# Spreading attention denominators over partitions: a DMA broadcast through DRAM in place of a TensorE matmul

## The chip, the cores and the metric

One NeuronCore of one Trainium2 chip runs the whole program. The metric is the device time of one execution in microseconds (us). "Faster" and "slower" mean by more than 2%. The kernel before takes 255.7 us.

A program on one core shows no second die to compare with, so the state of a run ("fast" or "slow") is told by its distance from the fastest run of the same kernel. A ratio is the mean time of one kernel's fast runs over that of the other's fast runs of the same rounds on the same chip, so it is not quite the ratio of the medians that are quoted.

## The reference, cut to what matters

```python
B, S, D, H = 1, 2048, 448, 16          # Dh = 28; N = 4 segments of L = 512
xn = layernorm(x)
for s in range(4):                      # attention with a memory carried from segment to segment
    p     = softmax(qs @ ks.T * scale + causal_mask)
    a_dot = p @ vs                                    # the kernel divides after the product
    num, den = phi(qs) @ M, phi(qs) @ z + 1e-6        # memory read
    o = g * num / den + (1 - g) * a_dot               # g = sigmoid(beta), per head
    M, z = M + phi(ks).T @ vs, z + sum(phi(ks))
out = x + (o @ wo) * silu((gelu(xn @ w_gate) * (xn @ w_up)) @ w_down)
```

Two divisions matter here: the softmax's, and `num / den`. The kernel does both late, as multiplications by inverses. Its products have 128 partitions = 4 heads x 32 rows (28 values, a denominator, padding) and 512 columns (tokens). The inverse of a head's 512 denominators is needed on all 32 partitions of that head.

## The kernel before: the parts that matter

```python
def evac(s, g, side, ps, copy=None):        # PSUM product to SBUF; its denominator rows by DMA to dc
    ...
    nc.sync.dma_start(out=dc[s, side][g * HG * RC:(g + 1) * HG * RC, :],
                      in_=t[Dh:P:HP, :].rearrange("i (c f) -> i c f", f=64))

def invert(s, side, g0=0, g1=G, to=None, eng=None, queues=None):
    ...                                     # VectorE: d = 1 / ((d + eps) * gate), 128 x 64, f32
    t = work.tile([P, 3, 64], BF16, name="terms")
    for i in range(3):                      # f32 as a sum of three bf16 terms
        eng.tensor_copy(out=t[p, i, :], in_=d)
        if i < 2:
            eng.tensor_tensor(out=d, in0=d, in1=t[p, i, :], op=ALU.subtract)
        queues[i].dma_start(out=rows[...][32 * i + g0 * HG:32 * i + g1 * HG, :]
                            .rearrange("h (c f) -> h c f", f=64), in_=t[p, i, :])

def inverses(s, side, g, at):               # TensorE spreads 4 heads' rows over 4 x 32 partitions
    r = ps_m.tile([P, L], F32, name="m")
    nc.tensor.matmul(out=r[:], lhsT=spread[:, g, :], rhs=rows[at][:], start=True, stop=True)
    return r[:]

# used by VectorE, 27 times:
nc.vector.tensor_tensor(out=dst, in0=o_n, in1=inverses(s, 1, g, 1), op=ALU.mult)   # scale_memory ("scl")
nc.vector.tensor_tensor(out=o_a, in0=o_a, in1=r, op=ALU.mult)                      # combine ("cmb")
# normalised x, one buffer per block of 128 tokens, transposed by DMA:
xn[b] = xns[b]                              # 4 buffers
nc.sync.dma_start_transpose(out=xnT[s][:, :, b * P:(b + 1) * P], in_=xn[b][:])
# the plan: in which slot of the program each small step is issued, found by search for this kernel
PLAN = {..., "inv3": 138, "cmb30": 144, "cmb31": 147, "cmb32": 149, ...}
```

The program goes: gate phase 0, attention 0, gate 1, attention 1, gates 2 and 3, attention 2, attention 3, the rest of the down projections and the output. A "gate phase" is the gate and up projections of one segment.

## Time and profile before

| | |
|---|---|
| time | 255.7 us (255.2 to 255.8) |
| TensorE, VectorE, ScalarE, GpSimd busy | 93%, 71%, 66%, 36% of a span of 253.9 us |
| chain that ended last | TensorE 75% |
| DMA | 15.07 MB, 27509 packets |

Read the chain first: it follows the work back from the last instruction, and its shares tell which engine's work made the time. Busy shares only tell which engines could not have been the limit. The lines themselves stand in the prediction.

### The profile page before, as it was taken

Reading aid. Unit: us, or ns where it says so; the run is one execution under the profiler, and the core shown is the slowest. Engines: PE = TensorE matmul, PEld = TensorE weight load, DVE = VectorE, ACT = ScalarE, POOL = GpSimd, SP = SyncE. Lnnn points to the kernel's source line nnn. Section 1 sums busy time; section 2 is a strip of 40 time slices with the busy share of each in tenths; the row PEclk is TensorE's granted clock in tenths of the full one; section 3 lists DMA queues with packets and bytes.
Section 4 is the critical chain, followed back from the end, with each engine's and each line's share of the span. In section 5 each row is a group of like instructions: output and inputs, shape, how many; then the busy total and the mean of one; then the engine's idle time right before and its main releaser. Section 6 shows DMA issues by size and latency. Waiting matters only on the chain.

```text
span 253.9 us, 4494 instructions
## 1 busy us (share of the span) xinstructions
PE 237.1 (93%) x1589; PEld 103.6 (41%) x1609; DVE 180.7 (71%) x362; ACT 167.5 (66%) x248; POOL 90.6 (36%) x195
## 2 busy tenths in 40 slices
PE   7899999999999999999999999999998999989970
PEld 7443333444344435444434334434433333334630
DVE  5877554827986857976698557536799866796990
ACT  5755878679995657679883575333897888884100
POOL 2500653443631322444532107040174545482030
PEclk9999999999999999999999999999999999999995
DMA  7999413200220135020120220000200010001111
GB/s 213 329 313 261 82 23 65 91 25 4 43 45 6 37 63 148 1 59 5 40 61 1 49 41 4 4 8 3 76 16 23 26 27 6 6 1 28 54 38 48
DMA packets 27509, 15.07 MB, mean 59 GB/s; under 512 B 17880, under 2 KB 26584, under 8 KB 27480
## 3 DMA queue, kind: packets, MB, share of 16 engines
q1 hardware_dynamic: 25276, 12.93, 20.6%
q10 hardware_dynamic: 2204, 1.79, 2.4%
q8 instruction: 14, 0.23, 0.4%
q14 instruction: 15, 0.12, 0.2%
HBM read 9.18 MB, written 1.84 MB: 43 GB/s over the span
## 4 chain that ended last, share of the span: by engine, by line
PE 75%; DVE 9%; ACT 7%; issue 4%; DMA 1%; POOL 1%; ACTq 0%
PE s L648 19%; PE m L689 15%; PE m L402 9%; PE s L496 5%; ACT pt L502 4%; PE pv L648 4%; PE m L648 4%; PE pv L515 4%; PE s L655 3%; PE m L441 3%; PE m L724 3%; PE m L573 2%; PE m L655 2%; DMA x_sb<-in_A_x_dram 1%; DVE hT L662 1%
## 5 line engine op out<-in xcount | busy, mean ns | idle before, releaser
L502 ACT ACTIVATE pt<-s 128x1024 bf16<-128x1024 f32 x80 | 77.5, 1024 | 16.1 <-PE s L496 12.6
L506 POOL TENSOR_SCALAR_AFFINE_SELECT pt<-pt 128x256 bf16<-128x256 bf16 x128 | 55.3, 452 | 63.4 <-ACT pt L502 60.4
L689 PE MATMUL m<-wd_sb,hT 128*128 128x448 bf16 x224 | 50.5, 353 | 0.2 <-DVE wu_sb L613 0.2
L662 DVE TENSOR_TENSOR hT<-gl,s 128x512 bf16<-128x512 bf16 x40 | 27.0, 680 | 9.0 <-ACT gl L661 8.6
L648 PE MATMUL s<-xnT,wg_sb 128*128 128x512 bf16 x118 | 32.3, 380 | 0.9 <-DVE hT L662 0.4
L648 PE MATMUL s<-xnT,wu_sb 128*128 128x512 bf16 x118 | 32.0, 379 | 0.1
L661 ACT ACTIVATE gl<-s 128x512 bf16<-128x512 f32 x40 | 23.7, 593 | 10.2 <-PE s L648 8.5
L689 PEld LDWEIGHTS <-hT 128*128 128x128 bf16 x224 | 20.4, 98 | 22.0 <-issue 4.0
L662 DVE TENSOR_TENSOR hT<-gl,pv 128x512 bf16<-128x512 bf16 x16 | 11.0, 688 | 24.9 <-ACT gl L661 24.9
L648 PEld LDWEIGHTS <-wu_sb 128*128 128x128 bf16 x168 | 16.4, 98 | 19.9 <-issue 0.2
L648 PEld LDWEIGHTS <-wg_sb 128*128 128x128 bf16 x168 | 15.2, 98 | 21.5 <-issue 6.0
L661 ACT ACTIVATE gl<-m 128x512 bf16<-128x512 f32 x16 | 9.4, 589 | 19.1 <-PE pv L655 19.1
L496 PE MATMUL s<-qT,kT 32*128 32x512 bf16 (+3 forms) x256 | 19.4, 300 | 1.9 <-ACT pt L502 1.9
L295 POOL TENSOR_TENSOR rstd<-rstd,nhalf 128x2 f32<-128x2 f32 (+1 forms) x8 | 5.4, 677 | 40.0 <-DVE rstd L293 40.0
L315 ACT ACTIVATE xn<-x_sb,shift,rstd 128x448 bf16<-128x448 bf16 (+1 forms) x24 | 12.7, 590 | 7.7 <-DVE shift L312 7.7
L402 PE MATMUL m<-xnT,wk_pad 128*128 128x512 bf16 x58 | 16.3, 379 | 1.1 <-DVE sg L727 0.5
L402 PE MATMUL m<-xnT,wq_pad 128*128 128x512 bf16 x60 | 16.6, 380 | 0.2
L441 PE MATMUL m<-wv_sb,xnT 128*128 128x448 bf16 x64 | 14.4, 353 | 1.3 <-DVE vaug L443 1.2
L695 ACT ACTIVATE th<-m 128x448 f32<-128x448 f32 x16 | 8.8, 550 | 8.6 <-PE m L689 8.6
L406 DVE CAST kT<-m 128x512 bf16<-128x512 f32 x16 | 10.9, 683 | 4.9 <-PE m L402 4.7
L496 PEld LDWEIGHTS <-kT 32*128 32x128 bf16 x256 | 5.6, 91 | 19.7 <-issue 19.3
L515 PE MATMUL pv<-pt,vaug 128*32 128x128 bf16 (+3 forms) x256 | 13.5, 303 | 0.0
(138 smaller groups left out, 360.6 us busy)
## 6 DMA issues: line engine op xcount, KB each, us to landing
x_sb<-in_A_x_dram SPq DMA_DIRECT2D x7, 224.0 KB
wd_sb<-in_B_w_down_dram SPq DMA_DIRECT2D x1, 1568.0 KB
wg_sb<-in_B_w_gate_dram SPq DMA_DIRECT2D x1, 1344.0 KB
wu_sb<-in_B_w_up_dram SPq DMA_DIRECT2D x1, 1344.0 KB
xr<-in_A_x_dram ACTq DMA_DIRECT2D x2, 448.0 KB
out_dram<-o_out SPq DMA_DIRECT2D x8, 112.0 KB
out_dram<-wq_pad SPq DMA_DIRECT2D x4, 112.0 KB
wo_sb<-in_A_wo_dram SPq DMA_DIRECT2D x4, 98.0 KB
```

Of the source, the lines that this page charges most:

```text
L315: nc.scalar.activation(out=xn[b][:, o], in_=xs[:, b, c], func=ACT.Identity, scale=rstd[:, b:b + 1], bias=shift[:])
L402: nc.tensor.matmul(out=pr[:], lhsT=wpad[nm][:, c, g * HG:(g + 1) * HG, :].rearrange("p h d -> p (h d)"), rhs=xnT[s][:, c, :], start=(c == ...
L441: nc.tensor.matmul(out=vp[:, 0:D], lhsT=xnT[s][:, c, b * P:(b + 1) * P], rhs=wv_sb[:, c, :], start=(c == 0), stop=(c == NDC - 1))
L496: nc.tensor.matmul(out=sp[i // 2][:, i % 2, c0:c0 + n], lhsT=kT[s][r, g, kb * P:(kb + 1) * P], rhs=qT[s][r, g, kb * P:L], start=True, stop ...
L502: nc.scalar.activation(out=pt[:, :, 0:w], in_=sp[pr][:, :, 0:w], func=ACT.Exp, scale=scale)
L506: nc.gpsimd.affine_select(out=v, in_=v, pattern=[[0, 2], [1, P]], compare_op=ALU.is_ge, fill=0.0, base=0, channel_multiplier=-1)
L515: nc.tensor.matmul(out=acc[i * HP:(i + 1) * HP, kb * P:L], lhsT=vaug[s % 2][:, kb, g * HG + i, :], rhs=pts[i // 2][:, i % 2, c0:c0 + n], s ...
L648: nc.tensor.matmul(out=gu[fc][i], lhsT=w_sb[:, c, fc * P:(fc + 1) * P], rhs=xnT[s][:, c, :], start=start and c == 0, stop=not start and c ...
L655: nc.tensor.matmul(out=gu[fc][i], lhsT=wg_sb[rs, NDC - 1, fc * P:(fc + 1) * P], rhs=xnT[s][rs, NDC - 1, :], start=start, stop=not start)
L661: nc.scalar.activation(out=gl[:], in_=g, func=ACT.Gelu_apprx_tanh)
L662: nc.vector.tensor_tensor(out=hT[s][:, fc, :], in0=gl[:], in1=u, op=ALU.mult)
L689: nc.tensor.matmul(out=d_ps[:, 0:D], lhsT=hT[s][:, fc, b * P:(b + 1) * P], rhs=wd_sb[:, fc, :], start=(fc == 0), stop=(fc == NFC - 1))
```

## The change

Intent: take 27 matmuls off the busiest engine. The f32 inverses go to a DRAM tile in one DMA, and each group's four rows are fetched into a 128 x 512 f32 tile in SBUF, every row read 32 times, up to three tiles ahead. To make room: three xn buffers in place of four, two output buffers in place of three, a late `unit` matrix. The closing multiplies and adds are reordered, and the plan is a new one. Cut to its core:

```diff
-    rows = [const.tile([P, L], BF16, name=f"rows{i}") for i in range(2)]
-    spread = const.tile([P, G, P], BF16, name="spread")
+    SPREAD = 3
+    sprp = pool("sprp", SPREAD)
+    drp = pool("drp", 3, space=DRAM)
@@ invert
-    (three bf16 terms, three DMAs to rows)
+    nc.sync.dma_start(out=t[g0 * HG:g1 * HG, :].rearrange("h (c f) -> (h c) f", f=64), in_=d)
+    for g in range(g0, g1):
+        wanted.append((plan[f"{'scl' if side else 'cmb'}{s}{g}"], len(wanted), s, side, g, t))
+    fetch()
+def fetch():
+    while wanted and len(spread) < SPREAD:
+        w = min(wanted)
+        wanted.remove(w)
+        s, side, g, t = w[2:]
+        b = spread[s, side, g] = sprp.tile([P, L], F32, name="spread")
+        nc.sync.dma_start(
+            out=b[:],
+            in_=t[g * HG:(g + 1) * HG, :].unsqueeze(1).to_broadcast([HG, HP, L]))
@@ inverses
-    nc.tensor.matmul(out=r[:], lhsT=spread[:, g, :], rhs=rows[at][:], start=True, stop=True)
+    return spread[s, side, g][:]        # after its use: spread.pop(...), fetch()
@@ normalised x
-    for i in range(NB):                 # xn buffers
+    for i in range(NB - 1):
-    xn[b] = xns[b]
+    xn[b] = xns[b % len(xns)]
@@ end
-    (multiply, multiply, add, multiply, multiply, add on VectorE; two adds on GpSimd)
+    (four multiplies first; adds 0 and 1 on GpSimd, then 2 and 3 on VectorE)
@@ PLAN (most of its entries move), for example
-    "inv3": 138, "cmb30": 144, "cmb31": 147, "cmb32": 149, "invm3": 113, "scl31": 120, "split3": 7
+    "inv3": 137, "cmb30": 143, "cmb31": 144, "cmb32": 144, "invm3": 111, "scl31": 115, "split3": 6
```

## The prediction

> **What bounds the kernel now.** I read the page first: busy shares, the 40 slices, the chain that ended last. Then I cut the span into stages (the view by windows), because a share over the span mixes stages with different limits.
>
> ```profile
> PE 237.1 (93%) x1589; PEld 103.6 (41%) x1609; DVE 180.7 (71%) x362; ACT 167.5 (66%) x248; POOL 90.6 (36%) x195
> PE   7899999999999999999999999999998999989970
> DVE  5877554827986857976698557536799866796990
> PE 75%; DVE 9%; ACT 7%; issue 4%; DMA 1%; POOL 1%; ACTq 0%
> PE s L648 19%; PE m L689 15%; PE m L402 9%; PE s L496 5%; ACT pt L502 4%; PE pv L648 4%; PE m L648 4%; PE pv L515 4%; PE s L655 3%; PE m L441 3%; PE m L724 3%; PE m L573 2%; PE m L655 2%; DMA x_sb<-in_A_x_dram 1%; DVE hT L662 1%
> ```
>
> TensorE is busy nearly everywhere but in the first and the last two slices, and three quarters of the chain are its matmuls. L573, the broadcast that the change removes, is itself 2% of the chain (2.2% in the chain told in order of time, 5.6 us). Now the stages, of all instructions and then of the broadcast's alone; the columns are the stretch, its length, and busy us with counts for each engine:
>
> ```profile
> 97.00:129.00 32.00, 31.79 (x249) 14.22 (x252) 25.23 (x46) 26.05 (x32) 14.07 (x31) 1.00 0.16 42
> 162.00:178.00 16.00, 15.89 (x92) 6.97 (x93) 8.77 (x15) 5.45 (x10) 3.15 (x7) 1.00 0.03 5
> 178.00:205.00 27.00, 25.61 (x200) 10.30 (x202) 24.42 (x45) 22.59 (x27) 12.49 (x28) 1.00 0.12 38
> 205.00:229.00 24.00, 22.47 (x196) 8.70 (x195) 17.89 (x32) 20.82 (x26) 14.02 (x32) 1.00 0.04 7
> 229.00:244.00 15.00, 15.00 (x99) 8.19 (x97) 12.44 (x28) 3.19 (x6) 1.53 (x4) 1.00 0.11 34
> ...
> 205.00:229.00 24.00, 2.76 (x8) 0.61 (x8) 0.00 (x0) 1.00 0.04 7
> ```
>
> Up to 178 us (gate phases and the first two attention segments) TensorE is the bound: 99% and nothing else near. In 178 to 205 VectorE is busy 24.4 of 27 us, and from 205 to 229 ScalarE's exponentials take 20.8 of 24; there the chain hops between engines. From 229 to 244 it is TensorE again, without a gap. So a matmul removed before 178 or after 229 should be time saved, and one removed between only in part.
>
> [...]its chain has six such matmuls in 1.29 us, 0.215 us each, at a granted clock of 1.00. So the mean of 385 ns that L573 shows is latency, not its price. [...] The trace has one case: the last denominator row's DMA starts to issue at 228.97 and VectorE, which waits for it, starts at 230.72: 1.75 us for 8 KB. [...] The new fetch has a source of 4 heads x 32 copies x 512[...]. No trace of before shows this shape. [...]the last adds take 1033 ns beside GpSimd's, the same kind 622 ns in the row that writes wq_pad.
>
> **The change, part by part.**
>
> ```profile
> L573 PEld LDWEIGHTS <-spread x27: 95/96/99, 90.4 to 239.5; 128*128 128x128 bf16 x27
> L573 PE MATMUL m<-rows,spread x25: 378/389/391, 90.4 to 239.7; 128*128 128x512 bf16 x25
> L559 POOL CAST terms<-dc x12: 237/237/238, 83.1 to 166.1; 128x64 bf16<-128x64 f32 x12
> L559 DVE CAST terms<-dc x9: 191/194/280, 203.4 to 232.6; 128x64 bf16<-128x64 f32 x6, 96x64 bf16<-96x64 f32 x3
> L561 DVE TENSOR_TENSOR dc<-dc,terms x6: 222/224/441, 203.7 to 232.3; 128x64 f32<-128x64 f32 x4, 96x64 f32<-96x64 f32 x2
> ```
>
> Removed on TensorE: 27 broadcasts (27 weight loads; two matmul records are missing). 27 x 0.215 = 5.8 us. By windows, counting weight loads: 15 before 178, 9 in 178 to 229, 3 after. I give the 15 and the 3 in full: 18 x 0.215 = 3.9. Of the other 9 (1.9 us) a third, because TensorE is only one of three engines that take turns there: 0.6. Sum 4.5 us saved.
>
> Removed on VectorE and GpSimd: the splitting into three bf16 terms. On GpSimd, 12 x 0.237 + 8 x 0.306 = 5.3 us, plus 2.7 us for the mask, all off the path (GpSimd is 36% busy). On VectorE 9 casts and 6 subtractions: 1.3 + 0.6 and 1.1 + 0.4 = 3.4 us by the groups kept apart by shape, all from 203 us on, where VectorE is one of the engines that take turns. I allow 0.6 us saved.
>
> Not changed in size: the 27 multiplies. They read the inverse from PSUM now at 0.68 us (L626, L613, L622); with both inputs in SBUF the nearest row is the combining add of f32 tiles, 0.69 us undisturbed and 0.93 where GpSimd was masking. GpSimd is busy about half the time in the attention stages, so perhaps 16 multiplies pay 0.1 us each on average: 1.6 us of VectorE work, of which I put 0.4 on the path.
>
> Added: 7 row writes to DRAM and 27 fetches of 128 x 2 KB, in place of 21 small DMAs. 27 x 256 KB is 7.1 MB on top of 15.07, mostly in stages where the DMA share is 0.03 to 0.2. Bandwidth is no issue; latency may be. From denominators to a usable tile: two VectorE operations (0.27 + 0.55), the row write (1.75), the fetch: 1.75[...] The new plan gives the first use, in slots after the inversion: 8, 7, 8, 3, 5, 4 and 6. A slot is 1.7 us in a gate phase (24 us for 14), 1.6, 1.35 and 1.2 us in the attention segments, near 0.7 in the closing part: 13, 11, 14, 5.2, 6, 5.4 and 4.2 us. The first three are covered. [...] VectorE has a quarter of its time free and TensorE works ahead through three PSUM buffers[...].
>
> **The tail.** Today VectorE does multiply, multiply, add, multiply, multiply, add, at 0.6 us a multiply and 1.03 an add; the third multiply sits behind an add although its matmuls are done. The change does the four multiplies first, the first two adds going to GpSimd. The last add then ends about 0.5 us earlier. The bf16 row DMA that now holds ScalarE's queue 1.4 us at 232.3 goes too; TensorE has no gap there, so I count nothing. The earlier GpSimd memsets and later weight padding at the start I count as nothing.
>
> **Sum:** -4.5 - 0.6 - 0.5 + 0.4 + 1.0 = -4.2; with the plan retuned (units of the down projection moved behind the last attention) perhaps 0.3 more. 255.7 - 4.5 = 251.2 us, 1.8% faster.
>
> **Rivals.** (1) Everything hides: fetches land in time, and the removed 5.8 us count in full with 0.6 and 0.5: 248.8 us. For it: TensorE has the largest share in every stage but one, and each broadcast also held one of three PSUM buffers. Against it: VectorE and ScalarE bind for 50 us. (2) A DMA wait takes the place of the broadcast: VectorE, in order, waits for late tiles, and the Sync queue, in order too, waits for a tile to be used before it issues the next fetch, holding the transposes and stores behind it; with two store buffers for three, that comes back to VectorE. [...] For it: [...]short leads late in the plan. Against it: that queue already waits long (33.5 us in total for the pk tiles) with no harm to the chain, and the leads were chosen anew. (3) VectorE becomes the bound by contention with GpSimd: 1.6 us on the path instead of 0.4: 252.4 us.
>
> **Range and chances.** From 248.8 (rival 1) to 255.0 (rival 2, most of it), 8 in 10. The 2% line is at 250.6, 0.6 us under my centre and well inside the range, so: faster 0.41, same 0.52, slower 0.07, the last for a stalled Sync queue that I can't see from here.
>
> **What would show it.** Right: no L573 group, TensorE's busy time about 6 to 9 us less, DMA near 22 MB, the stretch before 178 us shorter by about 3, waits of VectorE for the new tile totalling 2 to 6 us and few of them on the chain, and the span ending some 6 us after VectorE's last add, as before (248.2 to 253.9). Wrong: waits of multiplies for the fetch that are followed by TensorE gaps (rival 2); two-input multiplies near 0.9 us and VectorE over 95% in the third attention segment (rival 3); or no VectorE wait at all (rival 1). If the stages before 178 us do not shrink, my reading that TensorE bounds them is what failed.

"Six such matmuls" are of 512 columns, and the "one case" is of the time from a DMA's issue to the engine that waits for it. The sum came to 251.2 us (255.7 - 4.5 - 0.6 - 0.5 + 0.4 + 1.0 - 0.3). Of its terms the reason for the 1.0 is a time for the fetch's transfer and the waits of VectorE worked out from it: no trace of before showed this shape of DMA, so the 1.0 us were my estimate and not shown. The other parts, 0.27 + 0.55 + 1.75 + 1.75 = 4.3 us with the 1.75 us of the 8 KB case for both DMAs, would alone have left 0.1 us of wait, at the shortest lead of 4.2 us. The order that rival 2 names is seen in that trace: the third closing multiply starts at 245.96, 1.2 us after its matmuls ended (244.72), when the add before it ends; and on the Sync queue a store whose data were ready at 129.02 is issued at 129.84, after a transpose (128.54 to 129.74).

## The result, and the profile after

The changed kernel takes 269.4 us (268.5 to 272.6; the highest of its four runs was a slow one and is not in the ratio), before 255.75 us in the same rounds: ratio 1.053, 95% interval 1.048 to 1.058. It is 5% slower, far above the 248.8 to 255.0 us that I gave.

The page of the changed kernel, the parts shown of before:

```profile
PE 236.8 (89%) x1582; PEld 101.4 (38%) x1582; DVE 175.7 (66%) x345; ACT 168.4 (63%) x248; POOL 85.3 (32%) x171
PE   6999798999999879999999879999989986588850
DVE  5877465667787177897976264655997445668572
PE 47%; DMA 27%; DVE 15%; ACT 4%; issue 3%; SPq 1%; POOL 1%; DVEq 0%; ACTq 0%
PE s L645 13%; DMA spread<-rows 13%; PE m L394 8%; DMA xnT<-xn 7%; PE m L686 7%; PE m L433 3%; PE s L488 3%; PE s L652 2%; PE pv L645 2%; DMA dc<-oU 2%; DVE hT L659 2%; PE m L645 2%; PE pv L507 2%; DMA rows<-dc 2%; ACT gl L658 1%
```

No compute engine became the limit; all shares fell. TensorE's busy time hardly fell, although 27 matmuls are gone (I had said 6 to 9 us less; with no fetch to wait for, in `nofetch` below, it is 232.8 us). It now has gaps in slices 14 and 15, 23 and 24 (counted from 1) and from 33 on. Six gaps of more than 1.2 us, in its timeline from 18 us on, add up to 12.3 us; before has none of that length there. After two of the six, of 2.6 and 1.7 us, the granted clock of TensorE fell to 0.50 (156 to 158, 234 to 237), and what follows is stretched: three matmuls of 512 columns took 1.46 us from 155.85 on, in place of 0.81. Two of 2.7 and 2.8 us, which ended at 95.0 and 255.7, left it at 1.00, so in this trace the length of a gap alone did not decide. What grew is DMA on the chain, from 1% to 27%: the new fetches (spread<-rows, 13%), but also the transposes of the normalised x (xnT<-xn, 7%), which the change does not touch. The long DMA pieces, in the chain in order of time (start us, length us):

```profile
84.57 8.04 DMA xnT<-xn
...
143.93 8.96 DMA xnT<-xn
...
209.10 6.70 DMA spread<-rows
...
230.27 7.04 DMA spread<-rows
...
244.71 9.47 DMA spread<-rows
```

The waits view (engine, line, what it waited for: us in total, times, longest):

```profile
DVE oU L622 <- DMA spread<-rows: 9.6, 6, 4.1
ACT xn L309 <- DMA xnT<-xn: 7.2, 2, 3.9
DVE dc L542 <- DMA dc<-oU: 5.5, 2, 4.2
DVE wu_sb L608 <- DMA spread<-rows: 5.3, 2, 4.0
DVE oU L608 <- DMA spread<-rows: 1.9, 2, 1.6
```

VectorE waits 16.9 us for fetched tiles (the tile's own view; the lines above are rounded); I had said 2 to 6. The last column but one of the windows view is the share of the core's 16 DMA engines that were busy, the last GB/s. Two stretches of the changed kernel in which little but fetches is under way:

```profile
226.00:230.00 4.00, 3.02 (x27) 1.11 (x20) 0.59 (x1) 3.61 (x4) 2.24 (x6) 1.00 0.25 98
250.00:254.00 4.00, 2.82 (x18) 1.65 (x15) 1.39 (x2) 0.54 (x1) 0.00 (x0) 1.00 0.26 81
```

A share of 0.25 is what 4 engines of 16 would give. (The share can pass 1: it is 2.24 in 86 to 87, beside a transpose. So it is read only where fetches run nearly alone.) The DMA view shows 104 GB/s over and over, 26 for each of four: a tile of 256 KB takes 2.5 us, three in a row 7.6 us.

Now the stages, from ScalarE's timelines (first gelu of gate phase 1, first exponential of attention 1, first gelu of gate phase 2, first exponential of attention 2, end of the span); the lower rows belong to the experiments:

| profiled run | start to gate 1 | gate 1 | attention 1 | gates 2, 3 | attention 2 to end | span |
|---|---|---|---|---|---|---|
| before | 75.3 | 23.7 | 33.2 | 48.5 | 73.3 | 253.9 |
| after | 75.3 | 26.0 | 32.2 | 51.6 | 81.8 | 266.9 |
| nofetch | 75.1 | 23.2 | 31.8 | 47.1 | 71.6 | 248.7 |
| xn4 | 75.1 | 23.2 | 34.6 | 47.1 | 82.0 | 262.0 |
| heads | 75.2 | 24.0 | 31.7 | 47.1 | 71.8 | 249.9 |
| tail_alone | 75.3 | 23.7 | 33.2 | 48.4 | 72.0 | 252.7 |

Each row is one profiled execution: two of heads (this one and that of heads_again) differ by 1.2 us in the last column, so smaller differences there mean little. The loss sits in the gate phases, which hold the transposes, and most of it (8.5 of 13.0 us) after the start of attention 2, where tiles are used soon after their inversion.

### The profile page after: what moved, and what is told of

Same layout as the page of the kernel before. It is cut to its first block, busy times and chain, and to the rows that moved or that the text cites. A ratio compares the mean times of both kernels' runs of the same rounds, so it can differ in the third digit from the quotient of the medians.

```text
span 266.9 us, 4408 instructions
## 1 busy us (share of the span) xinstructions
PE 236.8 (89%) x1582; PEld 101.4 (38%) x1582; DVE 175.7 (66%) x345; ACT 168.4 (63%) x248; POOL 85.3 (32%) x171
## 4 chain that ended last, share of the span: by engine, by line
PE 47%; DMA 27%; DVE 15%; ACT 4%; issue 3%; SPq 1%; POOL 1%; DVEq 0%; ACTq 0%
PE s L645 13%; DMA spread<-rows 13%; PE m L394 8%; DMA xnT<-xn 7%; PE m L686 7%; PE m L433 3%; PE s L488 3%; PE s L652 2%; PE pv L645 2%; DMA dc<-oU 2%; DVE hT L659 2%; PE m L645 2%; PE pv L507 2%; DMA rows<-dc 2%; ACT gl L658 1%
## 5 line engine op out<-in xcount | busy, mean ns | idle before, releaser
L498 POOL TENSOR_SCALAR_AFFINE_SELECT pt<-pt 128x256 bf16<-128x256 bf16 x128 | 58.5, 477 | 64.9 <-ACT pt L494 63.3
L686 PE MATMUL m<-wd_sb,hT 128*128 128x448 bf16 x224 | 52.0, 362 | 0.0
L645 PE MATMUL s<-xnT,wg_sb 128*128 128x512 bf16 x120 | 33.3, 387 | 1.3 <-DVE hT L659 1.3
L645 PE MATMUL s<-xnT,wu_sb 128*128 128x512 bf16 x120 | 33.1, 385 | 0.0
L658 ACT ACTIVATE gl<-s 128x512 bf16<-128x512 f32 x40 | 23.6, 592 | 12.3 <-PE s L645 9.6
L645 PEld LDWEIGHTS <-wu_sb 128*128 128x128 bf16 x168 | 16.6, 99 | 23.2 <-issue 4.0
L645 PE MATMUL pv<-xnT,wu_sb 128*128 128x512 bf16 x48 | 13.0, 379 | 2.7 <-DVE hT L659 2.7
L652 PE MATMUL s<-xnT,wg_sb 64*128 64x512 bf16 x80 | 12.6, 383 | 3.1 <-DVE hT L659 3.1
L622 DVE TENSOR_TENSOR oU<-oU,spread 128x512 f32<-128x512 f32 x11 | 8.0, 728 | 9.6 <-DMA spread<-rows 9.6
## 6 DMA issues: line engine op xcount, KB each, us to landing
spread<-rows SPq DMA_DIRECT2D x27, 256.0 KB
```

The costliest lines, as they stand in the source:

```text
L498: nc.gpsimd.affine_select(out=v, in_=v, pattern=[[0, 2], [1, P]], compare_op=ALU.is_ge, fill=0.0, base=0, channel_multiplier=-1)
L645: nc.tensor.matmul(out=gu[fc][i], lhsT=w_sb[:, c, fc * P:(fc + 1) * P], rhs=xnT[s][:, c, :], start=start and c == 0, stop=not start and c ...
L652: nc.tensor.matmul(out=gu[fc][i], lhsT=wg_sb[rs, NDC - 1, fc * P:(fc + 1) * P], rhs=xnT[s][rs, NDC - 1, :], start=start, stop=not start)
L658: nc.scalar.activation(out=gl[:], in_=g, func=ACT.Gelu_apprx_tanh)
L686: nc.tensor.matmul(out=d_ps[:, 0:D], lhsT=hT[s][:, fc, b * P:(b + 1) * P], rhs=wd_sb[:, fc, :], start=(fc == 0), stop=(fc == NFC - 1))
```

## The experiments

My theory (A): the fetch, whose slowest dimension is 4, runs on four engines (the share of 0.25 above); that makes it slow (104 GB/s) and makes everything that shares those engines late. Rivals: (B) the way through DRAM and the queue's order cost the time, whatever the number of engines; (C) the xn buffer taken away holds ScalarE; (D) reading the same DRAM row 32 times is slow; (E) the new plan leaves too little time.

### Four or two copies of each row in DRAM

`wide16`: each row is written four times, so that a fetch reads 16 rows 8 times each. `wide8` has 2 for 4.

```diff
-    drp.tile([H, L], F32, name="rows")
+    drp.tile([H, 4, L], F32, name="rows")
-    nc.sync.dma_start(out=t[g0 * HG:g1 * HG, :].rearrange("h (c f) -> (h c) f", f=64), in_=d)
+    for r in range(4):
+        nc.sync.dma_start(out=t[g0 * HG:g1 * HG, r, :].rearrange("h (c f) -> h c f", f=64), in_=d)
-    in_=t[g * HG:(g + 1) * HG, :].unsqueeze(1).to_broadcast([HG, HP, L])
+    in_=t[g * HG:(g + 1) * HG].rearrange("h r l -> (h r) l").unsqueeze(1)
+         .to_broadcast([HG * 4, HP // 4, L])
```

> The changed kernel with each row written to DRAM four times (four small row writes for one), so that a fetch reads 16 rows x 8 copies: its slowest dimension is 16 in place of 4; bytes, buffers, plan and queue are the same. Theory A (a fetch of 4 heads x 32 copies runs on four DMA engines only, so 256 KB takes some 3 us of those engines, three in a row 9.5 us, and transposes queue behind them): the wait for the last three fetches falls from 9.5 us to below 5, the transposes' wait of 8 to 9 us disappears, and the time falls from 269 to 251 to 255 us. Rival B (the latency of the way through DRAM and the Sync queue's order cost the time, whatever the number of engines): 265 us or more. Rival C (the fourth xn buffer that the change took away holds ScalarE): part only, 260 to 266 us, with ScalarE's wait for the transpose still there.

> The same with two row copies: slowest dimension 8. Theory A: the wait for the last three fetches about half of 9.5 us, the time between the changed kernel and the 16-row form, 255 to 260 us. Rival B: 265 us or more, as both others.

Measured: wide16 256.0 us (ratio to before 1.002, interval 1.000 to 1.004), wide8 255.3 us (1.001, 0.996 to 1.005). wide16 is 1 us above my range, wide8 within it. Some 13 us of the change's time come back with the same fetched bytes, SBUF buffers, queue and plan. While the last fetches run, the windows view has for wide8 and then for wide16:

```profile
238.00:241.00 3.00, 2.90 (x19) 1.78 (x17) 1.82 (x4) 0.54 (x1) 0.00 (x0) 1.00 0.51 173
239.00:241.00 2.00, 2.00 (x13) 1.25 (x12) 1.53 (x3) 0.08 (x1) 0.00 (x0) 1.00 1.04 272
```

The share is 0.26 in the change, 0.51 in wide8 and 1.04 in wide16, as 4, 8 and 16 engines of 16 would give. After the start of attention 2, the chain of wide16 has these fetch pieces:

```profile
204.92 3.31 DMA spread<-rows
...
218.15 3.31 DMA spread<-rows
...
236.31 3.11 DMA spread<-rows
```

3.1 and 3.3 us in place of 5 to 9.5, and the transposes behind fetches take 3.0 and 3.9 us in place of 8 to 9. Rival B falls as the main cause. The last fetch on the chain lies in order: 9.5 us on 4 engines, 6.2 in wide8, 3.1 in wide16. The total time of wide8 should have lain between too, and does not: it is that of wide16 within the noise. Part of what more engines bring goes into the further row writes, which come before each first fetch: from the first row write to the first fetch it takes 3.9 us in wide16, 2.5 in wide8 and 1.5 in the change (at 80 us). That this is what evens them out is not shown. VectorE's waits for tiles stayed: 14.3 us in wide16, 11.9 in wide8, against 16.9. So most of what came back is not VectorE's own waiting; I take it to be the delay of other DMAs and of TensorE behind the fetches.

### No fetch at all

`nofetch` gives a wrong result: the multiplies read one constant SBUF tile, the row writes stay.

```diff
-    sprp = pool("sprp", SPREAD)
+    ones = const.tile([P, L], F32, name="ones_l")      # memset once
 def fetch():
-    ...
+    pass
-    return spread[s, side, g][:]
+    return ones[:]
```

> Wrong result on purpose: the changed kernel without any fetch, all 27 multiplies reading one constant tile in SBUF; the row writes stay. This is the floor of the change: TensorE's 27 broadcasts gone and no DMA wait. If my step that TensorE's removed time is saved holds, 249 to 251 us; if the removed matmuls were worth little, 253 to 256 us; if the plan, the smaller buffers or contention of two-SBUF multiplies with GpSimd cost time by themselves, above 256 us.

Measured: 250.7 us (250.0 to 253.7), ratio 0.985 (0.978 to 0.991). So my sum without the fetches is met within the interval, which is wide (250 to 253 us). That each part of it was right (matmuls, order of the tail, plan, buffers) one run can't show; but no large cost of the plan or the smaller buffers is left where no fetch is waited for. The fetches cost the change 269.4 - 250.7 = 18.7 us by the medians, 17.4 by the ratios, 18.2 by the two profiles.

### The fourth xn buffer given back

`xn4`; the second output buffer borrows that xn buffer, at a time when it is free.

```diff
-    outp = pool("outp", 2)
+    outp = pool("outp", 1)
-    for i in range(NB - 1):
+    for i in range(NB):                                  # xn buffers
-    o_out = o2_out[:, b, :] if s == 2 else outp.tile([P, D], BF16, name="o_out")[:]
+    o_out = (o2_out[:, b, :] if s == 2 else xns[NB - 1][:, 0:D] if b % 2
+             else outp.tile([P, D], BF16, name="o_out")[:])
```

> The changed kernel with the fourth xn buffer given back (the second output buffer borrows it later to make room). Theory A: ScalarE's waits for a transpose (3.3 and 3.9 us) go, but the fetches stay slow: 262 to 267 us. Rival C (the lost buffer is the main cost): below 260 us.

Measured: 264.7 us (ratio 1.039, 1.034 to 1.043), 4.7 us less than the change by the medians, 3.7 by the ratios. ScalarE's wait for transposes is gone, and gates 1, 2 and 3 are as long as in nofetch; 2.9 us more in attention 1 take part of it back. The last stage keeps its 82.0 us. So C is real but about a quarter of the loss, and with fast fetches it vanishes (heads_xn4, below), so it is a consequence of A. With three buffers, ScalarE must wait for the first transpose of a group before it can write the fourth block. In the changed kernel it waits 3.3 us for this, until 92.69, and its next gelu starts at 93.69, after it. With fast fetches the same three buffers cost little: ScalarE waits 2.2 us in wide16 and 2.4 in heads (below). The timeline of the Sync queue (SPq) in the changed kernel shows what the transposes stand behind:

```profile
81.38 1.70 SPq L560 DMA_DIRECT2D spread<-rows  x3
83.18 1.29 SPq L525 DMA_DIRECT2D dc<-oU  x2
84.57 3.47 SPq L315 DMA_TRANSPOSE xnT<-xn  x2
```

Three fetches are issued from 81.4 on. Their traffic starts in 82 to 83, and at 2.5 us each they hold their four engines until about 91: the share is back at 0.26 and 0.24 from 89 to 91. The transpose issued at 84.57 is done at 92.6.

### One fetch per head

`heads`: one row copy as in the change, four DMAs per tile, each of one row read 32 times.

```diff
-    nc.sync.dma_start(
-        out=b[:],
-        in_=t[g * HG:(g + 1) * HG, :].unsqueeze(1).to_broadcast([HG, HP, L]))
+    for i in range(HG):
+        nc.sync.dma_start(
+            out=b[i * HP:(i + 1) * HP, :],
+            in_=t[g * HG + i:g * HG + i + 1, :].to_broadcast([HP, L]))
```

> The changed kernel with each fetch cut into four DMAs, one per head: one row of 2 KB in DRAM read 32 times, slowest dimension 32[...]; one row copy as in the change, the same bytes, but four issues of some 0.5 us for one. Theory A (number of engines): close to the forms with row copies, 253 to 259 us, the issues costing something. Rival D (the forms with copies were fast because their reads spread over more DRAM rows, not over more engines): the reads of one row stay slow, 265 us or more.

> The per-head fetches once more, for the interval and beside the others: 251.5 to 253.5 us, 1 to 1.6% below the kernel before.

Measured: 252.4 us (ratio 0.987, 0.984 to 0.990), and on the next chip 252.6 us (0.988, 0.986 to 0.990). It is 17 us faster than the change, better than the 253 to 259 us that I expected, and 1.2% below the kernel before: clear of noise, though within the 2% that count as the same. It reads one DRAM row 32 times, so D falls. It goes through DRAM on the same queue with the same bytes, so B falls as well. Its chain, in order of time (last fetches), and the Sync queue's timeline for the last twelve issues:

```profile
204.59 2.01 DMA spread<-rows
...
215.40 1.96 DMA spread<-rows
...
221.65 2.17 DMA spread<-rows
```

```profile
230.25 5.41 SPq L561 DMA_DIRECT2D spread<-rows  x12
```

On the chain, a piece now lands 2.0 to 2.2 us after its issue begins. The price is issue: 12 DMAs take 5.4 us of the Sync queue. VectorE's waits for tiles are 6.6 us.

### What is left: the plan

`wide8_lead` is, against its name, the wide8 kernel once more; `w8_late_use` is the one with later uses:

```diff
-    "scl20": 91, "scl21": 98, "scl22": 88, "scl23": 103, "scl30": 117, "scl31": 115, "scl32": 120, "scl33": 122,
+    "scl20": 90, "scl21": 94, "scl22": 90, "scl23": 98, "scl30": 121, "scl31": 120, "scl32": 125, "scl33": 125,
-    "cmb20": 124, "cmb21": 128, "cmb22": 128, "cmb23": 129, "cmb30": 143, "cmb31": 144, "cmb32": 144,
+    "cmb20": 126, "cmb21": 129, "cmb22": 130, "cmb23": 129, "cmb30": 144, "cmb31": 147, "cmb32": 149,
```

> The form with two row copies once more, one look, on this chip beside the others: 254 to 257 us.

> The form with two row copies, and the uses of the last two segments' inverses put back to the slots of the plan of before (later by 0 to 10 slots for the memory side, 0 to 5 for the combining). Theory E (what is left between the fast fetch, 255.3 us, and no fetch at all, 250.7 us, is uses planned too soon after their inversion): VectorE's waits for the fetches fall from about 12 us in total to below 6, and the time to 252 to 254 us. If the rest is row writes and busy queues, 255 us or more.

Measured: 255.3 us in the one look, and 256.2 us (254.1 to 257.9; ratio of its three fast runs 0.998, 0.992 to 1.005). VectorE's waits fell as expected, to 4.4 us in its profile, but that profile fell in a slow run and the time did not move: E is not shown. A wait taken off VectorE by later use is not time gained here. (The expectation's "0 to 10 slots later" was loose: three of the memory side's slots are earlier.)

`oldplan` is the changed kernel under the whole plan of before, `before_newplan` the kernel before under the whole plan of the change; the edit swaps the table `PLAN`.

> The changed kernel, four-engine fetches and all, under the whole plan of before (its inversions are 2 slots later or 3 earlier, its uses later in segments 2 and 3). If the short leads of the new plan were the main cause, this recovers most: below 260 us. If slow fetches are, whatever the plan, 263 to 271 us.

> The kernel before, with TensorE's broadcasts, under the plan of the change. If the new plan by itself costs time, it is slower here too: 257 us or more (its leads are short for the three bf16 row DMAs as well). If the plan is neutral: 255 to 257 us.

Measured: oldplan 280.4 us (ratio 1.094, 1.087 to 1.101), before_newplan 267.5 us (1.045, 1.042 to 1.049). oldplan is beyond both of my ranges; before_newplan is in the first ("257 us or more"), but by far more than I had thought. The short leads of the new plan are not what made the late stage slow: with the later uses of the old plan, the stretch from attention 2 to the end takes 81.4 us against 81.8. The further 11 us of oldplan lie earlier. Of these, 4.0 us are lost up to gate 1, before any fetch is issued (the first at 88.6): there ScalarE waits 2.6 us for a transpose before it can write one of the three xn buffers, for which the old plan was not made. In gate 1 it is 7.0 us. So oldplan tests the buffers together with the leads. In these two pairs each plan fits its own kernel. The TensorE form under the new plan has its loss after the start of attention 2 (82.9 us against 73.3). There, waits that the DMA form puts on VectorE stand on TensorE itself, as in this line of TensorE's timeline, whose bracket is the idle time before it and what ended it:

```profile
210.98 0.38 PE L573 MATMUL m<-rows,spread 128*128 128x512 bf16 x1 [2.07 <-DMA rows<-terms]
```

This explains 2 of the 12 us. Another gap, of 1.9 us, ends at 192.95 (on a VectorE multiply), and after both gaps the granted clock was 0.50 for two to three us (195 to 197, 212 to 215). In the first of these stretches four matmuls of 448 columns (L724) took 1.70 us from 195.50 on, against 0.92 from 203.27 on. The rest of that difference stays open.

### The two remaining parts

`tail_alone` is the kernel before with only the new order of the closing operations; `heads_xn4` joins heads and the fourth xn buffer.

```diff
 # tail_alone, against before
-    for b in range(NB):
-        (multiply b; add b on VectorE if b is odd, on GpSimd if even; store)
+    for b in range(NB):
+        nc.vector.tensor_tensor(out=ts[b], in0=ts[b], in1=acc[b // 2][:, b % 2, 0:D], op=ALU.mult)
+        if b < 2:
+            last_add(b, nc.gpsimd)
+    for b in range(2, NB):
+        last_add(b, nc.vector)
```

> The kernel before with only the new order of the closing multiplies and adds. My step said 0.5 us: a ratio of 0.998. If GpSimd's second add in a row ends later than VectorE's did, 1.000 or above.

> Per-head fetches and the fourth xn buffer. In the run without it ScalarE still waited 2.4 us for transposes before it could write an xn buffer. Where that wait counts, 1 to 2 us less than without: 250.5 to 252 us. Where it is hidden: the same within 0.5 us.

Measured: tail_alone 254.4 us, ratio 0.996 (0.994 to 0.998): the reorder is worth 1.0 us by the ratio (0.5 to 1.6 by its interval), so the 0.5 that I had put lies at the edge. VectorE's closing timeline, before:

```profile
244.99 1.04 DVE L967 TENSOR_TENSOR wv_sb<-wg_sb,x_sb 128x448 bf16<-128x448 f32 x1
245.96 1.14 DVE L965 TENSOR_TENSOR wg_sb<-wg_sb,s 128x448 f32<-128x448 f32 x2
247.13 1.03 DVE L967 TENSOR_TENSOR wv_sb<-wg_sb,x_sb 128x448 bf16<-128x448 f32 x1
```

and in tail_alone:

```profile
245.71 1.15 DVE L970 TENSOR_TENSOR wg_sb<-wg_sb,s 128x448 f32<-128x448 f32 x2 [0.74 <-PE s L960]
246.78 1.15 DVE L966 TENSOR_TENSOR wv_sb<-wg_sb,x_sb 128x448 bf16<-128x448 f32 x2
```

The last two adds take 1.15 us together, where one took 1.03 beside GpSimd's. VectorE still ends only 0.2 us earlier (247.9 against 248.2), so most of the gain lies in the stores after it; these traces don't show where. heads_xn4 takes 252.2 us, ratio 0.986 (0.984 to 0.989), against 0.988 for heads in the same rounds: no difference clear of noise. With fast fetches the lost buffer costs nothing that can be seen. These two are the best versions found, 1.2 to 1.4% below the kernel before.

## Why the prediction was wrong, by its own steps

**What held.** TensorE was the bound before 178 us, and matmuls removed there are time saved: 15 x 0.215 = 3.2 us were foretold, and up to the start of attention 2 nofetch is 180.65 - 177.11 = 3.5 us shorter. (In the change itself that stretch is 4.5 us longer. By my own sign this would have meant that TensorE did not bound it; nofetch shows that the fetches hid the gain.) The floor by my sum, without the fetch term, was 255.7 - 4.5 - 0.6 - 0.5 + 0.4 - 0.3 = 250.2 us; measured 250.7. Inside it some terms may have been too large: after that point nofetch is shorter by 1.7 us, the reorder alone by 1.2 in its profile. That leaves 0.5 us for the 12 other broadcasts and VectorE's splitting, for which I had put 0.6 + 0.65 + 0.6; but single profiles differ by as much, so this is a hint and not shown. If it is so, the closeness of my sum is partly luck. In the trace the new fetch took a share of 0.25 of the engines, as four of 16 would give, and moved 104 GB/s.

**The step that failed** is the term for added latency, the 1.0 us in the sum, my estimate. Measured, the fetches cost some 18 us over the form without them (18.7 by the medians), and VectorE's waits for tiles were 16.9 us, where I had said 2 to 6. Three things were wrong in it.

First, I worked out a wait for the first tile of each inversion only. I had written a time for each further tile fetched at once, and then did not add it; measured, it is 2.5 us. In the closing part the third tile is the one that counts: its multiply starts 9.5 us after its issue, and the output projection stands behind it. The stretch from attention 2 to the end grew from 73.3 to 81.8 us, where the form without fetches has 71.6.

Second, I let VectorE's free quarter hide the waits. It is an average over the span. In the late stages the chain goes from the fetch to the multiply to the evacuation to the next denominators (the pieces at 209, 230 and 244 us above), so waits add up instead of being absorbed.

Third, I looked for what the fetches wait for and not for what waits behind them. On the Sync queue I named transposes held back by the order of issue. What the runs show is transposes already issued that land late, 8.0 and 9.0 us after their issue, and with one xn buffer fewer this stops ScalarE and then TensorE. I did not mention that buffer at all; giving it back recovers some 4 us (4.7 by the medians, 3.7 by the ratios).

**The rivals.** Rival 2 named the right kind of loss, a DMA wait in place of the broadcast, but its ceiling (cut) was taken from the same faulty estimate; the range with it ended at 255.0 us. Rival 1's 248.8 us is 2 us below what was measured with no fetch at all. Rival 3 was not the matter: in attention 2 (185 to 212 us) VectorE was busy 21.9 of 27 us, and its 27 multiplies took 20.1 us in place of 18.2, near the 1.6 us more that I had put.

**The plan.** I allowed 0.3 us for it. Swapping plans costs 11 to 12 us either way, so a plan is part of the kernel that it was found for.

## What to carry to other kernels

Look at the share of the DMA engines that each DMA on or near the path keeps busy: here a broadcast of 4 rows over 128 partitions used a quarter of them (share 0.25; 0.51 and 1.04 when it read 8 and 16 rows), and cutting it into four one-row DMAs with 32 copies each was worth 17 us of 269 with no byte saved. Price a transfer by the last tile of a burst (here used 9.5 us after its issue) and by what else must pass the same engines (here transposes that landed 8.0 and 9.0 us after theirs, against 3.0 and 3.9 in wide16), not by the first tile alone. And measure the floor (the operation replaced by something that is always ready) before judging an idea: here it showed that the idea was worth 1.5% and its one DMA pattern cost 7%.
